# Attention of the next batch inside the feed-forward stream: windowed attention and SwiGLU in one kernel

## Chip, cores and metric

One core of one Trainium2 chip. The metric is the device time of one execution in microseconds (us), median over runs.

## What is computed

```python
# q, k, v: (4, 8, 768, 64) float32 = batch B, heads H, sequence S, head width D
scores = (q @ k^T) / sqrt(64) + bias            # per batch and head
# key j is kept for query i if j < 8 (global) or 0 <= i - j < 96 (local)
# bias = -slope[h] * (96 if global and not local, else i - j); other keys: -1e9
a = softmax(scores)
x = (a @ v) with heads side by side             # (3072 tokens, 512)
g = x @ w_gate                                  # w_gate, w_val: (512, 1536)
out = ((g * sigmoid(g)) * (x @ w_val)) @ w_out  # w_out: (1536, 512); out: (3072, 512) float32
```

## The kernel before

Matmul operands are fp16, accumulation is float32 in PSUM. There are two stages, one after the other, each with its own PSUM pool (`psA`, then `psB`).

**Attention** runs over the 4 batches and over 4 pairs of heads in each. The loads of q, k and v go out on POOL's queue (`issue_in_dmas`) and cast to fp16 on the way; a row of a q or k load is 64 floats, 256 bytes. A batch has 16 q and k loads of 768 such rows and one v load of 6,144. The three weights follow the loads of batch 1. For a pair, `issue_qk_transposes` turns q and k with 12 matmuls against the identity (L150, L153), and VectorE copies the two results out of PSUM (L156, L157); this is done one pair ahead. Scores are computed transposed, keys on the partitions: per head six tiles of a chunk of 128 keys by up to 256 queries (L200, L205) and one of the first chunk by the last 512 queries (L209), for the 8 global keys. ScalarE takes the exponential (L221, L223, L225), VectorE multiplies with a mask of exponentials of the bias (L229). For the sums, the attention weights are the stationary operand and v with a column of ones the moving one (L236), which gives 6 blocks of 128 queries by 65 columns; VectorE takes reciprocals (L243) and products (L244). `issue_x_transposes` turns the result again (L164) into `xT`, feature-major, for the next stage (L166).

**Feed-forward** runs over 6 tiles of 512 tokens. For each of 12 blocks of 128 hidden features: 4 gate matmuls (L259), 4 value matmuls (L264), a sigmoid on ScalarE (L269), and two products on VectorE (L271, L272). Then 4 blocks of 128 tokens get 12 output matmuls each (L276), an eviction on ScalarE (L281) and a store (L282).

The order on each engine is planned by the framework's scheduler.

## Time and profile before

| | us |
|---|---|
| median of 3 runs | 361.26 (360.68 to 361.34) |
| span of the profiled execution, first to last instruction | 357.6 |
| up to the first transpose | 12.0 |
| attention | 153.8 |
| feed-forward, first to last matmul | 187.9 |
| after the last matmul | 3.9 |

Over the span TensorE is busy for 308.0 us, VectorE for 175.4, ScalarE for 126.5, POOL for 64.8. Busy times are sums over stages that have different limits, so the stages are to be read one by one. The granted TensorE clock is a share of 2.4 GHz; 0.50 is 1.2 GHz.

### The profile page before, as it was taken

What the parts mean: (1) busy time and instruction counts of PE and PEld (TensorE: products, weight loads), DVE (VectorE), ACT (ScalarE), POOL (GpSimd) and SP (SyncE); (2) the same over time, 40 slices, a digit from 0 to 9 for tenths busy, and PEclk for the clock granted to TensorE, in tenths of its full rate; (3) what the DMA queues carried; (4) which work ended last, traced back from release to release, by engine and by line L of the source; (5) the groups of instructions that cost most, each with busy time, mean ns of one, the idle gap of its engine ahead of it and who ended that gap; (6) DMA issues with size and microseconds to landing.
All of it is one profiled execution on the core that took longest, in us unless ns stands there. A gap on an engine that the chain in (4) does not pass through costs nothing.

```text
span 357.6 us, 4597 instructions
## 1 busy us (share of the span) xinstructions
PE 308.0 (86%) x1856; PEld 160.9 (45%) x1856; DVE 175.4 (49%) x288; ACT 126.5 (35%) x194; POOL 64.8 (18%) x76
## 2 busy tenths in 40 slices
PE   0447888787888788776999999999999999999995
PEld 0325555455555455443444444444444444444442
DVE  0217555535555555542871575178158418706740
ACT  1125444434444544533331332333133233313321
POOL 7659560195920000000000000000000000000000
PEclk9999555556555655555999999999999999999999
DMA  7999999999990000000001100200110020011002
GB/s 292 165 122 115 127 198 211 194 124 132 119 122 1 2 0 2 0 2 0 0 2 59 60 0 22 98 0 2 59 59 2 29 88 2 1 73 46 0 29 89
DMA packets 81333, 23.66 MB, mean 66 GB/s; under 512 B 75552, under 2 KB 77088, under 8 KB 81184
## 3 DMA queue, kind: packets, MB, share of 16 engines
q0 software_dynamic: 77424, 14.16, 71.3%
q1 hardware_dynamic: 3888, 9.21, 6.9%
q8 instruction: 14, 0.23, 0.3%
q14 instruction: 7, 0.06, 0.1%
HBM read 31.23 MB, written 6.29 MB: 105 GB/s over the span
## 4 chain that ended last, share of the span: by engine, by line
PE 53%; DVE 1%; ACT 1%; issue 0%; ACTq 0%
PE gps L259 18%; PE vps L264 17%; PE ops L276 17%; ACT AT L221 0%; PE outq L236 0%; DVE AT L229 0%; PE xtp L164 0%; ACT osb L281 0%; DVE xT L166 0%; DVE xs L244 0%; ACT AT L223 0%; PE scB L205 0%; PE scB L209 0%; DVE rqi L243 0%; ACTq L281 0%
## 5 line engine op out<-in xcount | busy, mean ns | idle before, releaser
L271 DVE TENSOR_TENSOR sl<-gps,sg 128x512 f32<-128x512 f32 x72 | 49.7, 691 | 72.0 <-ACT sg L269 71.9
L259 PE MATMUL gps<-xT,wg 128*128 128x512 f16 x288 | 74.8, 383 | 0.6 <-DVE xT L166 0.6
L264 PE MATMUL vps<-xT,wv 128*128 128x512 f16 x288 | 74.3, 381 | 0.0
L269 ACT ACTIVATE sg<-gps 128x512 f32<-128x512 f32 x72 | 43.0, 597 | 74.8 <-PE gps L259 74.8
L276 PE MATMUL ops<-wo,hT 128*128 128x512 f16 x288 | 63.1, 379 | 0.0
L272 DVE TENSOR_TENSOR hT<-vps,sl 128x512 f16<-128x512 f32 x72 | 49.7, 692 | 7.6 <-PE gps L259 0.5
L221 ACT ACTIVATE AT<-scA 128x1024 f16<-128x1024 f32 x32 | 32.7, 1023 | 53.4 <-issue 35.2
L259 PEld LDWEIGHTS <-wg 128*128 128x128 f16 x288 | 28.3, 98 | 34.9 <-issue 1.4
L264 PEld LDWEIGHTS <-wv 128*128 128x128 f16 x288 | 28.3, 98 | 34.6 <-issue 1.1
L276 PEld LDWEIGHTS <-hT 128*128 128x128 f16 x288 | 28.2, 98 | 34.0
L200 PE MATMUL scA<-qk 64*128 64x256 f16 x128 | 31.3, 390 | 11.2 <-ACT AT L225 10.6
L150 PE MATMUL trq<-ident,qst 128*128 128x128 f16 x96 | 14.8, 295 | 25.3 <-DMA qst<-in_q_dram 18.2
L229 DVE TENSOR_TENSOR AT<-AT,masks 128x1408 f16<-128x1408 f16 x32 | 28.5, 890 | 11.8 <-ACT AT L223 11.8
L281 ACT COPY osb<-ops 128x512 f32<-128x512 f32 x24 | 14.0, 585 | 53.5 <-PE ops L276 53.5
L108 POOL DMA_DIRECT2D kst<-in_k_dram x32 | 27.4, 879 | 28.4 <-DMA vpp<-in_v_dram 15.1
L236 PE MATMUL outq<-vpp,AT 128*128 128x65 f16 x480 | 30.8, 238 | 1.8 <-DVE AT L229 1.5
L236 PEld LDWEIGHTS <-AT 128*128 128x128 f16 x480 | 26.4, 127 | 11.7 <-DVE AT L229 6.8
L223 ACT ACTIVATE AT<-scB 128x384 f16<-128x384 f32 x32 | 15.7, 490 | 39.7 <-PE scB L209 39.7
L108 POOL DMA_DIRECT2D qst<-in_q_dram x32 | 27.3, 883 | 6.3 <-DMA wg<-in_moe_w_gate_dram 5.4
L243 DVE RECIPROCAL rqi<-outq 128x6 f32<-128x6 f32 x32 | 6.3, 196 | 38.7 <-PE outq L236 38.7
L150 PEld LDWEIGHTS <-qst 128*128 128x128 f16 x96 | 9.6, 127 | 34.0 <-DMA qst<-in_q_dram 19.1
L200 PEld LDWEIGHTS <-qk 64*128 64x128 f16 x128 | 14.3, 121 | 22.0 <-issue 16.0
(24 smaller groups left out, 169.4 us busy)
## 6 DMA issues: line engine op xcount, KB each, us to landing
out_dram<-osb SPq DMA_DIRECT2D x24, 256.0 KB, 2.0
qst<-in_q_dram POOLq DMA_DIRECT2D x32, 96.0 KB, 9.6
kst<-in_k_dram POOLq DMA_DIRECT2D x32, 96.0 KB, 9.3
vpp<-in_v_dram POOLq DMA_DIRECT2D x4, 768.0 KB, 11.5
masks<-attn_masks SPq DMA_DIRECT2D x1, 2816.0 KB, 9.4
wg<-in_moe_w_gate_dram POOLq DMA_DIRECT2D x1, 1536.0 KB, 11.8
wv<-in_moe_w_val_dram POOLq DMA_DIRECT2D x1, 1536.0 KB, 18.4
wo<-in_moe_w_out_dram POOLq DMA_DIRECT2D x1, 1536.0 KB, 25.3
```

The lines of the kernel that those rows point to most:

```text
L108: nc.gpsimd.dma_start(out=st[:, hp, :, hi, :], in_=src[b, 2 * hp + hi].rearrange("(j p) d -> p j d", p=128))
L150: nc.tensor.transpose(trq[:, 128 * j:128 * j + 128], qst4[:, hp, j, :], ident)
L200: nc.tensor.matmul(scA[:, col:col + n], lhsT=kT[:, 128 * ck:128 * ck + 128], rhs=qT[:, q0:q0 + n], start=True, stop=True)
L221: nc.scalar.activation(out=AT[:, 0:1024], in_=scA, func=AF.Exp, scale=float(scale))
L229: nc.vector.tensor_mul(AT[:, 0:1408], AT[:, 0:1408], masks[:, h, :])
L236: nc.tensor.matmul(oq3[:, jq, :], lhsT=AT[:, at_col:at_col + 128], rhs=vpp[:, bh * NT + ck, 0:65], start=(i == 0), stop=(i == len(cl) - 1))
L259: nc.tensor.matmul(gps, lhsT=wg[:, c, 128 * f:128 * f + 128], rhs=xT[c][:, 512 * tb:512 * tb + 512], start=(c == 0), stop=(c == NC - 1))
L264: nc.tensor.matmul(vps, lhsT=wv[:, c, 128 * f:128 * f + 128], rhs=xT[c][:, 512 * tb:512 * tb + 512], start=(c == 0), stop=(c == NC - 1))
L269: nc.scalar.activation(out=sg, in_=gps, func=AF.Sigmoid)
L271: nc.vector.tensor_mul(sl, gps, sg)
L272: nc.vector.tensor_mul(hT[:, f, :], vps, sl)
L276: nc.tensor.matmul(ops, lhsT=hT[:, f, 128 * t4:128 * t4 + 128], rhs=wo[:, f, :], start=(f == 0), stop=(f == NFF - 1))
```

## The change

Everything in the kernel is new but the loops' arithmetic.

- **Order.** The scheduler's order is replaced by the order written in the program (`manual_schedule`). Batch 0's attention runs first, in 12 rounds in which up to three pairs take one step each. From then on the program is a row of 96 slots: a slot has the 8 gate and value matmuls of one block of one 384-token tile (`gate_val`), three output matmuls of the tile before (`out_part`), and one step of attention of the next batch (`attention`), two steps ahead of the slot number. A pair has six steps: transposes, three of scores, two of values. Batches 1 to 3 have 72 steps, two of which stand ahead of slot 0.
- **Loads.** q and k are loaded with 6 tokens a partition, so that a row is 1,536 bytes; a q or k load of one batch is split at first (2, 2 and 4 heads) and whole later. v comes in 7 chunks plus 7 small loads. The weights are loaded in parts. All stay on POOL's queue: q and k of batch 0 for four heads, v of batch 0, the other four heads, wg and wv in four parts, wo in three, q and k of batch 1, v of batch 1. Those of batches 2 and 3 stand in the slots.
- **Chunks of keys.** A chunk is 8 global keys and 120 keys in order, against a window of 216 queries; there are 7. Global keys count for the first 120 queries of a window, so each query meets them once. The seven windows lie in three banks of 432 columns, and the two heads of a pair are computed in turn, one on each half of the array's rows.
- **Masks** are made on the chip, by the exponential of a table of distances, 864 columns a head, before and during batch 0's attention.
- **Values.** v (or a block of ones) is stationary with 64 columns, the weights move, and the two heads write the two halves of the partitions. The result is already feature-major, and the second transposes fall away. The sums of weights come out 64 times; VectorE transposes them in blocks of 32, takes 11 or 13 reciprocals, and transposes back.
- **Engines.** In the stream POOL multiplies with the masks and with the reciprocals (after a copy of the numerator by ScalarE); in batch 0 VectorE does. ScalarE copies q out of PSUM.
- **Gate.** Sigmoid becomes tanh: (tanh(g/2) + 1) * g in one VectorE instruction, and the factor of a half is in the eviction.

The core of the diff (added lines and lines in common):

```diff
+    def load_qk(b, h0, h1):
+        for st, src in ((qst[b], q), (kst[b], k)):
+            nc.gpsimd.dma_start(
+                out=st[:, h0:h1, :],
+                in_=src[b, h0:h1].rearrange("h (p j) d -> p h (j d)", p=128))
+    def load_v(b, c):
+        if c < NCH:
+            n = min(KC, S - KC * c)
+            nc.gpsimd.dma_start(
+                out=vS[NG:NG + n, b, c, :, :],
+                in_=v[b, :, KC * c:KC * c + n, :].rearrange("h p d -> p h d"))
+        else:
+            for cc in range(NCH):
                 nc.gpsimd.dma_start(
+                    out=vS[0:NG, b, cc, :, :],
+                    in_=v[b, :, 0:NG, :].rearrange("h p d -> p h d"))
...
+    def load_w(g):
+        f0 = WF * g
+        for w, src in ((wg, moe_w_gate), (wv, moe_w_val)):
             nc.gpsimd.dma_start(
+                out=w[:, :, f0:f0 + WF],
+                in_=src[:, f0:f0 + WF].rearrange("(c p) f -> p c f", p=128))
+    def load_wo(g):
+        nc.gpsimd.dma_start(
+            out=wo[:, 4 * g:4 * g + 4, :],
+            in_=moe_w_out[512 * g:512 * g + 512].rearrange("(f p) d -> p f d", p=128))
+    xT = sb.tile([128, NC, TOK], FP16, name="xT")
+    attn_tags = ["a0", "a1", "a2"]
+    pro_tags = ["a0", "a1", "a2", "g0", "g1", "v0", "v1", "o0"]
+    state = {"tags": pro_tags, "n": 0}
...
+    def make_masks(h):
+        nc.scalar.activation(out=masks[:, h, :], in_=dist, func=AF.Exp, scale=-slopes[h])
...
+        def transposes(self):
+            b, hp = self.b, self.hp
+            trq = bank("trq", FP16, S)
+            trk = bank("trk", FP16, S)
+            for st, tr in ((qst[b], trq), (kst[b], trk)):
+                for j in range(J):
+                    for hi in range(2):
+                        nc.tensor.transpose(
+                            tr[64 * hi:64 * hi + 64, 128 * j:128 * j + 128],
+                            st[:, 2 * hp + hi, D * j:D * j + D], ident)
+            self.qT = sb2.tile([128, S], FP16, name="qT", tag="qT")
+            self.kT = kTs[hp % 2]
+            nc.scalar.copy(
+                out=self.qT.rearrange("r (p j) -> r p j", j=J),
+                in_=trq.rearrange("r (j p) -> r p j", j=J))
+            k3 = self.kT.rearrange("r (c m) -> r c m", m=128)
+            t3 = trk.rearrange("r (j p) -> r p j", j=J)
+            for c0, c1, n in ((0, 6, KC), (6, 7, S - 6 * KC)):
+                nc.vector.tensor_copy(
+                    out=k3[:, c0:c1, NG:NG + n].rearrange("r c (p j) -> r c p j", j=J),
+                    in_=t3[:, 20 * c0:20 * c0 + (c1 - c0) * (n // J), :].rearrange(
+                        "r (c p) j -> r c p j", c=c1 - c0))
+            nc.vector.tensor_copy(
+                out=k3[:, :, 0:NG],
+                in_=k3[:, 0, NG:2 * NG].unsqueeze(1).broadcast_to([128, NCH, NG]))
+        def scores(self, bk, mul_eng):
+            hp = self.hp
+            sc = [bank("scA"), bank("scB")]
+            for c in range(NCH):
+                cb, col, q0, n = chunks[c]
+                if cb != bk:
+                    continue
+                for hi in range(2):
+                    r = slice(64 * hi, 64 * hi + 64)
+                    nc.tensor.matmul(
+                        sc[hi][:, col:col + n],
+                        lhsT=self.kT[r, 128 * c:128 * c + 128],
+                        rhs=self.qT[r, q0:q0 + n], start=True, stop=True)
             for hi in range(2):
+                at = sb2.tile([128, BANK], FP16, name="at", tag=f"at{hi}{bk}")
+                nc.scalar.activation(out=at, in_=sc[hi][:, 0:BANK], func=AF.Exp, scale=scale)
+                self.at[hi, bk] = at
             for hi in range(2):
+                at = self.at[hi, bk]
+                mul_eng.tensor_mul(at, at, masks[:, 2 * hp + hi, WIN * bk:WIN * bk + BANK])
+        def values(self, half, norm):
+            b, hp = self.b, self.hp
+            lo, hi_q = HALF[half]
+            n_q = hi_q - lo
+            num = bank("num")
+            den = bank("den")
+            parts = []
+            for c in range(NCH):
+                cb, col, q0, n = chunks[c]
+                a, z = max(q0, lo), min(q0 + n, hi_q)
+                if a < z:
+                    parts.append((c, cb, col + a - q0, a - lo, z - a))
+            for dst, ones_side in ((den, True), (num, False)):
+                for i, (c, cb, col, o, n) in enumerate(parts):
+                    for hi in range(2):
+                        r = slice(64 * hi, 64 * hi + 64)
                         nc.tensor.matmul(
+                            dst[r, o:o + n],
+                            lhsT=ones if ones_side else vS[:, b, c, 2 * hp + hi, :],
+                            rhs=self.at[hi, cb][:, col:col + n],
+                            start=(i == 0), stop=(i == len(parts) - 1),
+                            skip_group_check=True)
+            dT = sb2.tile([128, 416], FP32, name="dT", tag="dT")
+            dR = sb2.tile([128, 13], FP32, name="dR", tag="dR")
+            rb = sb2.tile([128, 416], FP32, name="rb", tag="rb")
+            nb = n_q // 32
+            nc.vector.transpose(dT[:, 0:n_q], den[:, 0:n_q])
+            nc.vector.reciprocal(
+                out=dR[:, 0:nb], in_=dT[:, 0:n_q].rearrange("p (n i) -> p n i", i=32)[:, :, 0])
+            nc.vector.transpose(
+                rb[:, 0:n_q].rearrange("p (n i) -> p n i", i=32),
+                dR[:, 0:nb].unsqueeze(2).broadcast_to([128, nb, 32]))
+            dst = xT[:, hp, b * S + lo:b * S + hi_q]
+            if norm == "vector":
+                nc.vector.tensor_mul(dst, num[:, 0:n_q], rb[:, 0:n_q])
+            else:
+                ns = sb2.tile([128, 416], FP32, name="ns", tag="ns")
+                nc.scalar.copy(out=ns[:, 0:n_q], in_=num[:, 0:n_q])
+                nc.gpsimd.tensor_mul(dst, ns[:, 0:n_q], rb[:, 0:n_q])
+    hTs = {}
+    def gate_val(t, f):
+        if f == 0:
+            hTs[t] = sb2.tile([128, NFF, TB], FP16, name="hT", tag="hT")
+        gps = ps.tile([128, 512], FP32, name="gps", tag=f"g{f % 2}")
+        vps = ps.tile([128, 512], FP32, name="vps", tag=f"v{f % 2}")
+        for w, dst in ((wg, gps), (wv, vps)):
             for c in range(NC):
                 nc.tensor.matmul(
+                    dst[:, 0:TB], lhsT=w[:, c, 128 * f:128 * f + 128],
+                    rhs=xT[:, c, TB * t:TB * t + TB],
                     start=(c == 0), stop=(c == NC - 1))
+        th = sb2.tile([128, TB], FP32, name="th", tag="th")
+        nc.scalar.activation(out=th, in_=gps[:, 0:TB], func=AF.Tanh, scale=0.5)
+        sl = sb2.tile([128, TB], FP32, name="sl", tag="sl")
+        nc.vector.scalar_tensor_tensor(
+            out=sl, in0=th, scalar=1.0, in1=gps[:, 0:TB], op0=AluOp.add, op1=AluOp.mult)
+        nc.vector.tensor_mul(hTs[t][:, f, :], vps[:, 0:TB], sl)
+    ops_t = {}
+    def out_part(t, i, part):
+        if part == 0:
+            ops_t[0] = ps.tile([128, 512], FP32, name="ops", tag="o0")
+        ops = ops_t[0]
+        for f in range(3 * part, 3 * part + 3):
+            nc.tensor.matmul(
+                ops, lhsT=hTs[t][:, f, 128 * i:128 * i + 128], rhs=wo[:, f, :],
+                start=(f == 0), stop=(f == NFF - 1))
+        if part == 3:
             osb = sb2.tile([128, DM], FP32, name="osb", tag="osb")
+            nc.scalar.mul(out=osb, in_=ops, mul=0.5)
+            r0 = TB * t + 128 * i
+            nc.sync.dma_start(out=out[r0:r0 + 128, :], in_=osb)
+    stage(0)
+    load_qk(0, 0, 2)
+    load_qk(0, 2, 4)
+    for c in range(NCH + 1):
+        load_v(0, c)
+    load_qk(0, 4, 8)
+    for g in range(4):
+        load_w(g)
+    for g in range(3):
+        load_wo(g)
+    stage(1)
+    load_qk(1, 0, 8)
+    for c in range(NCH + 1):
+        load_v(1, c)
+    pairs = {(b, hp): Pair(b, hp) for b in range(B) for hp in range(NP)}
+    make_masks(0)
+    make_masks(1)
+    for t in range(6 + 2 * (NP - 1)):
+        for hp in range(NP):
+            s = t - 2 * hp
+            if 0 <= s < 6:
+                if s == 1 and hp + 1 < NP:
+                    make_masks(2 * hp + 2)
+                    make_masks(2 * hp + 3)
+                pairs[0, hp].step(s, nc.vector, "vector")
+    state["tags"] = attn_tags
+    state["n"] = 0
+    todo = [(b, hp, s) for b in range(1, B) for hp in range(NP) for s in range(6)]
+    AHEAD = 2
+    loads = {}
+    for b in range(2, B):
+        base = 24 * (b - 2) + 2
+        loads[base] = [lambda b=b: (stage(b), load_qk(b, 0, 8))]
+        for c in range(NCH + 1):
+            loads.setdefault(base + 1 + c, []).append(lambda b=b, c=c: load_v(b, c))
+    def attention(i):
+        if i < len(todo):
+            b, hp, s = todo[i]
+            pairs[b, hp].step(s, nc.gpsimd, "gpsimd")
+    for i in range(AHEAD):
+        attention(i)
+    NT = TOK // TB
+    for t in range(NT):
+        for f in range(NFF):
+            i = NFF * t + f
+            for fn in loads.get(i, []):
+                fn()
+            gate_val(t, f)
+            if t > 0:
+                out_part(t - 1, f // 4, f % 4)
+            attention(i + AHEAD)
+    for i in range(3):
+        for part in range(4):
+            out_part(NT - 1, i, part)
 # ---- launch: one core; inputs and outputs as the reference has them ----
 _INS = ['q', 'k', 'v', 'n_global', 'n_local', 'moe_w_gate', 'moe_w_val', 'moe_w_out']
 _OUTS = [((3072, 512), 'float32')]
 _NUMBERS = {'n_global': 8, 'n_local': 96}
```

## Rows read from the trace of the kernel before

**Rows 1.** The page's slices, 40 of 8.94 us: busy tenths, granted clock in tenths.

```profile
PE   0447888787888788776999999999999999999995
PEclk9999555556555655555999999999999999999999
DMA  7999999999990000000001100200110020011002
```

**Rows 2.** Stretches: length, busy us (instructions) of PE, PEld, DVE, ACT, POOL; clock; DMA.

```profile
0.00:12.00 12.00, 0.00 (x0) 0.00 (x0) 0.00 (x0) 1.28 (x1) 7.17 (x13) 1.00 1.05 268
12.00:165.80 153.80, 120.16 (x993) 76.34 (x994) 76.22 (x144) 66.91 (x96) 57.59 (x64) 0.60 1.63 91
165.80:353.70 187.90, 187.82 (x864) 84.60 (x863) 99.22 (x144) 57.73 (x97) 0.00 (x0) 0.99 0.09 33
353.70:357.60 3.90, 0.00 (x0) 0.00 (x0) 0.00 (x0) 0.58 (x1) 0.00 (x0) 0.79 0.19 69
```

**Rows 3.** The chain that ended last, feed-forward: start us, us, what.

```profile
186.99 0.86 PE vps L264 x4
187.86 10.36 PE ops L276 x48
```

**Rows 4.** POOL in order of time: start us, us, instruction, [idle before, releaser].

```profile
1.24 1.78 POOL L108 DMA_DIRECT2D qst<-in_q_dram  x2 [0.80 <-POOLq L301]
...
23.66 0.83 POOL L108 DMA_DIRECT2D kst<-in_k_dram  x1 [3.97 <-DMA vpp<-in_v_dram]
...
43.33 0.82 POOL L108 DMA_DIRECT2D kst<-in_k_dram  x1 [3.79 <-DMA vpp<-in_v_dram]
...
56.23 0.82 POOL L108 DMA_DIRECT2D qst<-in_q_dram  x1 [5.41 <-DMA wg<-in_moe_w_gate_dram]
63.63 0.82 POOL L108 DMA_DIRECT2D kst<-in_k_dram  x1 [6.58 <-DMA wv<-in_moe_w_val_dram]
71.24 0.82 POOL L108 DMA_DIRECT2D kst<-in_k_dram  x1 [6.79 <-DMA wo<-in_moe_w_out_dram]
```

**Rows 5.** All engines in order of time, at half clock.

```profile
37.02 0.83 PE L153 MATMUL trk<-ident,kst 128*128 128x128 f16 x6
```

**Rows 6.** Weight loads of TensorE in order of time, at full clock.

```profile
28.35 0.33 PEld L200 LDWEIGHTS <-qk 64*128 64x128 f16 x4 [0.18 <-PE outq L236]
28.89 0.17 PEld L150 LDWEIGHTS <-qst 128*128 128x128 f16 x3 [0.21 <-issue]
...
29.35 0.55 PEld L236 LDWEIGHTS <-AT 128*128 128x128 f16 x15
...
30.90 0.34 PEld L164 LDWEIGHTS <-xs 128*128 128x128 f16 x6 [0.57 <-DVE xs L244]
31.34 0.09 PEld L200 LDWEIGHTS <-qk 64*128 64x128 f16 x1
```

**Rows 7.** Groups by line: count | busy us, mean ns | idle before, releaser.

```profile
L221 ACT ACTIVATE AT<-scA 128x1024 f16<-128x1024 f32 x32 | 32.7, 1023 | 53.4 <-issue 35.2 <-PE scA L200 15.9 <-ACT AT L225 2.2
...
L229 DVE TENSOR_TENSOR AT<-AT,masks 128x1408 f16<-128x1408 f16 x32 | 28.5, 890 | 11.8 <-ACT AT L223 11.8
...
L244 DVE TENSOR_TENSOR xs<-outq,rqi 128x384 f16<-128x384 f32 x32 | 17.8, 557 | 1.1
...
L223 ACT ACTIVATE AT<-scB 128x384 f16<-128x384 f32 x32 | 15.7, 490 | 39.7 <-PE scB L209 39.7
...
L281 ACT COPY osb<-ops 128x512 f32<-128x512 f32 x24 | 14.0, 585 | 53.5 <-PE ops L276 53.5
...
L156 DVE COPY qk<-trq 128x768 f16<-128x768 f16 x16 | 8.9, 557 | 24.5 <-PE trq L150 14.1 <-PE scB L209 10.4
...
L243 DVE RECIPROCAL rqi<-outq 128x6 f32<-128x6 f32 x32 | 6.3, 196 | 38.7 <-PE outq L236 38.7
...
L269 ACT ACT_TABLE_LOAD x1 | 1.3, 1283 | 5.7 <-PE gps L259 5.7
...
L119 POOL MEMSET vpp<- 128x192 f16 x1 | 1.0, 975 | 0.0
```

More of the change, by code (lines that the diff above doesn't have):

```diff
@@ L14, with _build_dist @@
 AF = mybir.ActivationFunctionType
-MASK_NEG = -30000.0
-def _build_consts(B, H, S, D, NG, NL):
-    slopes = 2.0 ** (-8.0 * (np.arange(H, dtype=np.float64) + 1) / H)
-    kk = np.arange(128)[:, None]
-    qq = np.arange(256)[None, :]
-    rel = qq - kk
-    is_local = (rel >= 0) & (rel < NL)
-    is_glob = kk < NG
-    keep0 = is_local | is_glob
-    dist0 = np.where(is_local, np.abs(rel), float(NL))
-    keepb = is_local
-    distb = np.abs(rel)
-    big = np.zeros((128, H, 1408), np.float16)
-    for h in range(H):
-        m0 = (np.exp(-slopes[h] * dist0) * keep0).astype(np.float16)
-        mb = (np.exp(-slopes[h] * distb) * keepb).astype(np.float16)
-        big[:, h, 0:256] = m0
-        for c in range(4):
-            big[:, h, 256 + 256 * c:512 + 256 * c] = mb
-        big[:, h, 1280:1408] = mb[:, 0:128]
-    bias0b = np.full((128, H), MASK_NEG, np.float32)
-    for h in range(H):
-        bias0b[:NG, h] = -float(NL) * slopes[h]
-    ident = np.eye(128, dtype=np.float16)
-    return big, bias0b, ident
+FAR = 60000.0
+KC = 120
+WIN = 216
+BANK = 432
+def _build_dist(S, NG, NL):
+    row = np.arange(128)[:, None]
+    col = np.arange(WIN)[None, :]
+    key = row - NG
+    rel = col - key
+    local = (rel >= 0) & (rel < NL) & (key >= 0)
+    inner = np.where(local, rel, FAR)
+    inner = np.where((row < NG) & (col < KC), NL, inner)
+    first = np.where(local, rel, FAR)
+    first = np.where(~local & (key >= 0) & (key < NG) & (col < KC), NL, first)
+    d = np.concatenate([first, inner, inner, inner[:, :168], inner[:, :48]], axis=1)
+    return d.astype(np.float16)
 @with_exitstack
@@ L69 @@
     assert (NG, NL) == (8, 96)
-    NT = S // 128
-    NBH = B * H
     NP = H // 2
@@ L118 @@
-    issue_in_dmas(0)
-    nc.gpsimd.memset(vpp[:, :, 64:65], 1.0)
-    xT = [sb.tile([128, TOK], FP16, name=f"xT{c}", tag=f"xT{c}") for c in range(NC)]
+    dist = sb.tile([128, 2 * BANK], FP16, name="dist")
+    nc.sync.dma_start(out=dist, in_=dist_dr.ap())
+    masks = sb.tile([128, H, 2 * BANK], FP16, name="masks")
+    ones = sb.tile([128, 64], FP16, name="ones")
+    nc.vector.memset(ones, 1.0)
+    kTs = [sb.tile([128, NCH * 128], FP16, name=f"kT{i}") for i in range(2)]
+    for t in kTs:
+        nc.vector.memset(t[:, 6 * 128 + 56:], 0.0)
@@ new lines, with stage @@
+    vS = sb.tile([128, B, NCH, H, D], FP16, name="vS")
+    nc.vector.memset(vS[:, :, 6, :, :], 0.0)
+    qst, kst = {}, {}
+    def stage(b):
+        qst[b] = sb2.tile([128, H, J * D], FP16, name="qst", tag="qst")
+        kst[b] = sb2.tile([128, H, J * D], FP16, name="kst", tag="kst")
+    def load_qk(b, h0, h1):
[3 more added lines that the diff above has]
+                in_=src[b, h0:h1].rearrange("h (p j) d -> p h (j d)", p=128))
@@ new lines, in load_wo, with bank @@
+    def load_wo(g):
[6 more added lines that the diff above has]
+    state = {"tags": pro_tags, "n": 0}
+    def bank(name, dt=FP32, cols=512):
+        tags = state["tags"]
+        tag = tags[state["n"] % len(tags)]
+        state["n"] += 1
+        return ps.tile([128, cols], dt, name=name, tag=tag)
@@ L262 @@
                     start=(c == 0), stop=(c == NC - 1))
-            for c in range(NC):
-                nc.tensor.matmul(
-                    vps, lhsT=wv[:, c, 128 * f:128 * f + 128],
-                    rhs=xT[c][:, 512 * tb:512 * tb + 512],
-                    start=(c == 0), stop=(c == NC - 1))
-            sg = sb2.tile([128, 512], FP32, name="sg", tag="sg")
-            nc.scalar.activation(out=sg, in_=gps, func=AF.Sigmoid)
-            sl = sb2.tile([128, 512], FP32, name="sl", tag="sl")
@@ L271 @@
-            nc.vector.tensor_mul(sl, gps, sg)
-            nc.vector.tensor_mul(hT[:, f, :], vps, sl)
-        for t4 in range(4):
-            ops = psB.tile([128, 512], FP32, name="ops", tag="ops")
-            for f in range(NFF):
-                nc.tensor.matmul(
-                    ops, lhsT=hT[:, f, 128 * t4:128 * t4 + 128],
-                    rhs=wo[:, f, :],
-                    start=(f == 0), stop=(f == NFF - 1))
-            osb = sb2.tile([128, DM], FP32, name="osb", tag="osb")
-            nc.scalar.copy(out=osb, in_=ops)
-            nc.sync.dma_start(
-                out=out[512 * tb + 128 * t4: 512 * tb + 128 * (t4 + 1), :],
-                in_=osb)
+        th = sb2.tile([128, TB], FP32, name="th", tag="th")
```

173 lines of the change are left out of this document (29 added, 144 removed).

## The prediction

> **What bounds the kernel now.** I read the slices first: TensorE is busy all along after the start, but its clock stands at half over most of the first half of the span, and the loads on the DMA engines end about where slice 12 does [rows 1]. The table of stretches gives the stages [rows 2]: 12.0 us of loads, 153.8 us of attention (TensorE busy for 120.2 of them, mean clock 0.60), 187.9 us of feed-forward (TensorE never idle, clock 0.99), and 3.9 us from the last matmul to the end, 357.6 in all. The runs' median is 361.26, so 3.7 us lie around the span; I add them at the end. The chain of waits shows that the feed-forward stage hangs on matmuls alone: four take 0.86 us, 48 take 10.36, so 216 ns for 512 columns [rows 3], 2.37 columns a nanosecond. Six tiles of 144 matmuls are 186.6 us of pure streaming; nothing of that can go. Attention hangs on no single engine: TensorE is idle 33.6 us there and at half clock most of the rest. What the change can win is the attention stage: three batches of four can lie inside a stage where VectorE and ScalarE idle [rows 2].
>
> **What is removed.** The 153.8 us stage as a stage, the 12.0 us wait for the first loads in part, and the second activation table load.
>
> **The start.** All loads stay on POOL's queue, and attention of batch 1 stands on TensorE ahead of the first feed-forward matmul, so the feed-forward stream begins only when batch 1's q and k have landed behind all weights. Row prices: a batch's 18,432 rows of 256 bytes (16 q and k loads of 768, one v of 6,144) take from 23.66 to 43.33, 1.07 ns a row; wo's 1,536 rows of 2,048 bytes take 7.61 us behind wv, 4.95 ns a row [rows 4]. A straight line between them gives 3.84 ns for the new 1,536-byte rows. Then: q and k of batch 0, 2,048 rows, 7.9; v, 6,592 rows of 256 bytes, 7.0; wg and wv, 4,096 rows, 15.7; wo 7.6; q and k of batch 1, 7.9: 46.1 us. From the first issue at 1.24, with some 2 us for the last landing, that is 49 to 50. POOL issues the 33 loads ahead at 0.83 each, 27 us, below that. Bounds: at wo's rate throughout 48; at the rate of the 256-byte rows 76.
>
> Batch 0's own attention starts near 6 and lies beside this. VectorE, a pair: copies 1.3 (below), six mask products at 0.38, twice two transposes, a reciprocal and a product, 3.8; 7.4, four pairs 30 us. TensorE at half clock takes 0.107 for 128 columns (six transposes in 0.83 with the tail of the last, [rows 5]), so 18 us for the 43,392 columns of four pairs if the two heads stream side by side and 36 if not. ScalarE has 23: eight masks of 864 elements at 0.89, 24 exponentials, four copies of q at 0.8. With the waits of twelve rounds I put its end at 46, not later than the loads; what hides it is the weights' transfer, and if it needs over 50 us the start moves with it. After q and k of batch 1 land, TensorE still has to transpose at half clock (24 x 0.107 = 2.6), wait for VectorE's copies (about 1.6), and do the first scores (0.4): the stream starts at **55** (bounds 53 and 80).
>
> **The stream.** Feed-forward columns are the same: 768 matmuls of 384 (162 ns) and 288 of 512 (216 ns), **186.6**. Between them lie 70 attention steps of 12 pairs. A pair has 24 transposes of 128 columns, 14 score matmuls with 2,592, and 32 value matmuls with 5,184: 10,848 columns. The trace shows matmuls only one after the other: 4.6 us at full clock, the upper bound. The two heads now use different halves of the array in turn; fully side by side it is 2.3 us, about what 70 weight loads need at the pace of the 15 loads in 0.55 (32 ns each, [rows 6]). No row says which; I take the middle, 3.45, 12 pairs 41.4, less the two steps done before: **40** (27 to 55).
>
> The Trainium skill (TensorEngine Tiling (Array Packing), Restrictions) says that column tiling does without fast weight loads; no row here has a column tile. By the Trainium skill's TensorE: Matmul & The Clock Gate (LDWEIGHTS: columns over 1.2 GHz) the 56 loads of 64 columns in a pair would be 3.0 us, an estimate, and with the scores the sum would be some 2 us more.
>
> Each step switches the array's shape twice. At full clock: four score matmuls from 28.35 stream until 28.78 and the next form loads at 28.89; six transposes from 30.90 end at 31.24 and the 64-row form loads at 31.34 [rows 6]. 0.10 each; 140 of them, **14** (12 to 28, if column tiles drain twice as long).
>
> Waits: VectorE's copies (557 ns for 768 contiguous elements; the new strided ones up to one element a cycle, 0.9, and two short ones at 0.2: 1.3) must end before the next step, 1.94 us of feed-forward later. Exponentials of 432 are 0.53, between L223's 490 ns for 384 and L221's 1,023 for 1,024; tanh of 384 is 0.49, the products of 384 are 0.56 (row L244) [rows 7]. Per pair, VectorE: 12 x 0.56, 1.3, and twice 1.3 is 10.6; ScalarE: six tanh, six exponentials, a 0.8 copy, two 0.49 copies and 1.5 evictions of 0.585 is 8.8. TensorE needs 6 x 1.94 + 3.45 + 1.2 = 16.3, so both lie beside it. POOL takes eight products a pair, six masks and two norms. Its only compute row is the strided memset, 975 ns for 192, which for 432 would be 2.2; VectorE's 890 for 1,408 would be 0.27. I take 1.3: 10.4, and with its DMA issues (32 of 0.9 over twelve pairs, 2.4) 12.8, still below 16.3. The steps that wait for POOL stand two slots, over 5 us, behind their scores. For what is late now and then (the first twelve slots have no output matmuls between, v of batch 1 lands about when it is wanted) I take half a microsecond a pair, **6** (0 to 12).
>
> At its start the clock is cold: stage 187.9 against 186.6, **1.3** [rows 2]. At the end 36 output matmuls share one bank: three evictions of about 0.85 with hand-over stand open, **2.5**. Sum: 55 + 186.6 + 40 + 14 + 6 + 1.3 + 2.5 = 305.4; the tail 3.9, around the span 3.7: **313 us**.
>
> **Rivals.**
> 1. *Loads at the price of short rows.* If 1,536-byte rows move at the rate of 256-byte ones, the stream starts at 80: 338 us. For it: the short rows carry 240 GB/s; against it: wo's 2,048-byte rows carry 413.
> 2. *POOL becomes the bound.* At 2.2 us a product, 20.0 a pair against 16.8 with waits: 12 x 3.2 more, 351 us. It bounds from 1.75 on, and eats the gain at 2.3. Against it: the memset writes single strided elements.
> 3. *Weight loads in line* (the one that ends slower). If in the tiled forms a load cannot be pulled ahead of the running matmul, each of 840 costs its 95 ns openly: 80 us, 393 us. It decides from 57 ns a load. Against it: the 64-row score loads are already pulled ahead [rows 6]; for it: no row has column tiles.
> 4. *The clock falls in the stream.* Attention ran at 0.60 though TensorE was busy for 120.2 of 153.8. Work done at half clock costs itself again; 48 us of the stream's 250 undo the gain, twice that gives 409. Against it: three quarters of the stream is feed-forward work, which held 0.99.
> 5. *Table loads in the stream.* The trace has a load of 1.283 us between exp and sigmoid. If tanh and exp share no table, each of 36 score slots has two: ScalarE 4.3 us against 2.65, 58 us, 371 us.
>
> On the last, the Trainium skill (ScalarE: Activation LUTs, Table sets: the hidden batching unit) lists tanh in exp's set, so there would be no load in the stream; no row here has a tanh.
>
> **Chances.** Forecast 0.64 (own range 300 to 330: start 53 to 60, attention 27 to 55); rival 1 0.10; rival 2 0.08, of which faster 0.06 and the same 0.01; rival 3 0.09, of which 0.01 faster and 0.01 the same, since part of the price may be hidden; rival 4 0.06, half of it faster; rival 5 0.03. Faster 0.64 + 0.10 + 0.06 + 0.01 + 0.03 = 0.84; same 0.02; slower 0.14. A measurement here tells about 0.2% from no change. The range, 290 to 345, reaches from a pair at 2.3 us with few waits to rival 1; rivals 3 and 5, most of 4 and the far end of 2 are outside.
>
> **What would show it.** Start: the first gate matmul near 55, with POOL's loads landed just before. Stream: granted clock 1.0, TensorE hardly idle, 2.4 to 3.3 us a slot, steps of a pair adding to 3 to 5 us; POOL's products at 1.0 to 1.6. One table load in the whole trace. Wrong it would be by gaps on TensorE released by POOL or by VectorE's copies, by pairs of matmuls that never overlap and loads in line, by a clock of 0.5 in the stream, or by a first gate matmul after 65.

## The result, and the profile after

The changed kernel takes **301.25 us** (median of 4 runs, 301.10 to 301.37) against 361.30 for the kernel before (4 runs, 360.68 to 362.73): a ratio of 0.833, 95% interval 0.831 to 0.835. The forecast was 313.

The slices of the page after, 40 of 7.48 us, answer to [rows 1]. TensorE is full from slice 8 on (slice 10, at 7, holds two value steps that wait), its clock is whole from there, and the loads ahead of the stream end with slice 7; slices 9 to 11 and 17 to 19 are the loads of batches 2 and 3.

```profile
PE   2528541599799999999999999999999999999983
PEclk9999755599999999999999999999999999999999
...
DMA  8989999909950010299501000100010000100111
```

The table of stretches after, cut at the first gate matmul and after the last matmul's start, answers to [rows 2] (same columns):

```profile
0.00:57.00 57.00, 23.11 (x308) 16.24 (x309) 29.40 (x75) 22.55 (x38) 32.38 (x47) 0.79 1.33 168
57.00:295.00 238.00, 233.10 (x1870) 125.27 (x1868) 149.99 (x297) 110.73 (x226) 120.51 (x133) 0.99 0.30 48
295.00:299.30 4.30, 0.33 (x2) 0.00 (x0) 0.00 (x0) 0.60 (x1) 0.00 (x0) 1.00 0.16 61
```

The span is 299.3: 57.0 of start, 238.0 of stream, 4.3 of end. In the stream TensorE is idle for 4.9 us and its clock stands at 0.99 of 2.4 GHz; VectorE (150), ScalarE (111) and POOL (121) have room. Before, 165.8 us passed ahead of the first feed-forward matmul [rows 2].

**The start.** TensorE in order of time after (start us, us, engine, line, what, [idle before, releaser]):

```profile
41.68 0.87 PE L238 MATMUL num<-at,vS 128*64 128x216 f16 x9
50.52 0.85 PE L182 MATMUL trq<-ident,qst 128*64 128x128 f16 x12 [7.97 <-DMA qst<-in_q_dram]
54.46 0.85 PE L182 MATMUL trk<-ident,kst 128*64 128x128 f16 x12 [3.09 <-DMA kst<-in_k_dram]
56.53 0.36 PE L210 MATMUL scA<-qT,kT 64*128 64x216 f16 x1 [1.22 <-DVE kT L197]
...
57.00 1.46 PE L272 MATMUL gps<-xT,wg 128*128 128x384 f16 x4
...
113.34 0.53 PE L182 MATMUL trq<-ident,qst 128*64 128x128 f16 x12
113.70 0.50 PE L182 MATMUL trk<-ident,kst 128*64 128x128 f16 x12
114.13 0.82 PE L272 MATMUL gps<-xT,wg 128*128 128x384 f16 x4
114.79 0.81 PE L272 MATMUL vps<-xT,wv 128*128 128x384 f16 x4
115.44 0.81 PE L291 MATMUL ops<-wo,hT 128*128 128x512 f16 x3
116.18 0.26 PE L210 MATMUL scA<-qT,kT 64*128 64x216 f16 x1
116.19 0.26 PE L210 MATMUL scB<-qT,kT 64*128 64x216 f16 x1
116.29 0.25 PE L210 MATMUL scA<-qT,kT 64*128 64x216 f16 x1
116.29 0.25 PE L210 MATMUL scB<-qT,kT 64*128 64x216 f16 x1
116.47 0.82 PE L272 MATMUL gps<-xT,wg 128*128 128x384 f16 x4
...
285.66 2.75 PE L291 MATMUL ops<-wo,hT 128*128 128x512 f16 x12 [0.69 <-ACT osb L296]
289.10 2.75 PE L291 MATMUL ops<-wo,hT 128*128 128x512 f16 x12 [0.69 <-ACT osb L296]
292.58 2.75 PE L291 MATMUL ops<-wo,hT 128*128 128x512 f16 x12 [0.73 <-ACT osb L296]
```

The top shows that batch 0's attention is over at about 42.5, and that TensorE then stands for 8 us until q of batch 1 has landed, and for 3 more until k has: 3.94 us between the two, for 1,024 rows, 3.85 ns a row.

**A slot.** The middle of that fence is one. Gate and value matmuls take 1.31 us (114.13 to 115.44), the output part 0.74 with a change of the array's shape behind it (116.18), a score step 0.29 (to 116.47), the transposes 0.79 (113.34 to 114.13). The scores of the two heads start 0 to 10 ns apart, and the next two 0.10 us later, about what 216 columns take alone at the feed-forward's rate (0.09, [rows 3]): the heads stream **side by side** at full rate. The start-to-start times of the six steps of a pair, each with the change back, are 0.79, 0.29, 0.29, 0.30, 0.59 and 0.79: 3.05 us. The bottom is the end: the last three output blocks wait 0.7 us each for the eviction of the bank they share.

The groups by line after, of the operations whose price had no row, or a row of another shape, in [rows 7]:

```profile
L278 ACT ACTIVATE th<-gps 128x384 f32<-128x384 f32 x96 | 47.5, 494 | 37.1 <-PE gps L272 36.7
L220 POOL TENSOR_TENSOR at<-at,masks 128x432 f16<-128x432 f16 x72 | 70.5, 1005 | 31.7 <-ACT at L216 31.6
L260 POOL TENSOR_TENSOR xT<-ns,rb 128x352 f16<-128x352 f32 (+1 forms) x24 | 24.1, 1005 | 26.1 <-DVE rb L251 26.0
L159 ACT ACT_TABLE_LOAD x1 | 1.3, 1283 | 0.7 <-PEq L376 0.7
```

POOL in order of time after, at the loads and where the stream begins:

```profile
15.15 0.55 POOL L123 DMA_DIRECT2D vS<-in_v_dram  x1 [0.60 <-DMA vS<-in_v_dram]
...
23.03 0.74 POOL L135 DMA_DIRECT2D wv<-in_moe_w_val_dram  x1 [0.59 <-DMA kst<-in_k_dram]
24.97 0.74 POOL L140 DMA_DIRECT2D wo<-in_moe_w_out_dram  x1 [1.20 <-DMA wg<-in_moe_w_gate_dram]
...
32.17 0.89 POOL L111 DMA_DIRECT2D qst<-in_q_dram  x1 [1.87 <-DMA wv<-in_moe_w_val_dram]
...
54.70 0.57 POOL L123 DMA_DIRECT2D vS<-in_v_dram  x1 [3.30 <-DMA kst<-in_k_dram]
...
59.74 1.10 POOL L123 DMA_DIRECT2D vS<-in_v_dram  x2 [0.50 <-DMA vS<-in_v_dram]
60.94 5.81 POOL L220 TENSOR_TENSOR at<-at,masks 128x432 f16<-128x432 f16 x6
```

POOL's queue issues batch 1's small loads of v until 60.84, though the first scores were there at 57, and then has six mask products in arrears. The rows up to 32.17 show how the queue is paced. In this program POOL does not issue a load before the one eight places ahead of it has landed: the 28th, at 23.03, waits for batch 0's last k, the 20th; the 29th for the first wg, the 21st; the 32nd for the second wv, the 24th. With them goes the busy share of the DMA engines over the first 60 us after, 40 slices of 1.5 us:

```profile
DMA  0699999993149999999999999999999999999994
```

It has a hole at 13.5 to 18 us. POOL is then at the end of v's seven small loads of batch 0, the last three of which wait for chunks of v to land, and the next large load, q of heads 4 to 7, is not issued before 15.70.

### The profile page after: what moved, and what is told of

Read it like the earlier page. It is cut to its first block, busy times and chain, and to the rows that moved or that the text cites. A ratio compares the mean times of both kernels' runs of the same rounds, so it can differ in the third digit from the quotient of the medians.

```text
span 299.3 us, 5659 instructions
## 1 busy us (share of the span) xinstructions
PE 256.5 (86%) x2176; PEld 141.5 (47%) x2176; DVE 179.4 (60%) x372; ACT 133.9 (45%) x265; POOL 152.9 (51%) x179
## 4 chain that ended last, share of the span: by engine, by line
PE 71%; DMA 16%; POOL 8%; DVE 2%; ACT 1%; issue 1%; POOLq 0%; ACTq 0%; DVEq 0%
PE gps L272 21%; PE ops L291 21%; PE vps L272 19%; DMA vS<-in_v_dram 7%; DMA wo<-in_moe_w_out_dram 5%; POOL at L220 3%; DMA wv<-in_moe_w_val_dram 3%; PE scA L210 3%; PE den L238 3%; PE num L238 2%; POOL vS L118 2%; PE trq L182 2%; PE trk L182 1%; POOL qst L111 1%; ACT osb L296 1%
## 5 line engine op out<-in xcount | busy, mean ns | idle before, releaser
L280 DVE SCALAR_TENSOR_TENSOR sl<-th,gps 128x384 f32<-128x384 f32 x96 | 52.9, 551 | 61.3 <-ACT th L278 61.3
L220 POOL TENSOR_TENSOR at<-at,masks 128x432 f16<-128x432 f16 x72 | 70.5, 1005 | 31.7 <-ACT at L216 31.6
L272 PE MATMUL gps<-xT,wg 128*128 128x384 f16 x384 | 79.8, 331 | 0.0
L272 PE MATMUL vps<-xT,wv 128*128 128x384 f16 x384 | 78.8, 328 | 0.0
L278 ACT ACTIVATE th<-gps 128x384 f32<-128x384 f32 x96 | 47.5, 494 | 37.1 <-PE gps L272 36.7
L282 DVE TENSOR_TENSOR hT<-vps,sl 128x384 f16<-128x384 f32 x96 | 53.5, 558 | 10.1 <-PE vps L272 0.2
L216 ACT ACTIVATE at<-scA 128x432 f16<-128x432 f32 x48 | 25.5, 532 | 37.9 <-PE scB L210 37.9
L260 POOL TENSOR_TENSOR xT<-ns,rb 128x352 f16<-128x352 f32 (+1 forms) x24 | 24.1, 1005 | 26.1 <-DVE rb L251 26.0
L118 POOL DMA_DIRECT2D vS<-in_v_dram x28 | 25.1, 909 | 10.9 <-DMA wo<-in_moe_w_out_dram 4.9
L216 ACT ACTIVATE at<-scB 128x432 f16<-128x432 f32 x48 | 25.5, 532 | 0.0
L210 PE MATMUL scA<-qT,kT 64*128 64x216 f16 (+2 forms) x112 | 18.7, 267 | 7.9 <-DVE kT L197 5.6
```

The lines of the kernel that those rows point to most:

```text
L118: nc.gpsimd.dma_start(out=vS[NG:NG + n, b, c, :, :], in_=v[b, :, KC * c:KC * c + n, :].rearrange("h p d -> p h d"))
L210: nc.tensor.matmul(sc[hi][:, col:col + n], lhsT=self.kT[r, 128 * c:128 * c + 128], rhs=self.qT[r, q0:q0 + n], start=True, stop=True)
L216: nc.scalar.activation(out=at, in_=sc[hi][:, 0:BANK], func=AF.Exp, scale=scale)
L220: mul_eng.tensor_mul(at, at, masks[:, 2 * hp + hi, WIN * bk:WIN * bk + BANK])
L260: nc.gpsimd.tensor_mul(dst, ns[:, 0:n_q], rb[:, 0:n_q])
L272: nc.tensor.matmul(dst[:, 0:TB], lhsT=w[:, c, 128 * f:128 * f + 128], rhs=xT[:, c, TB * t:TB * t + TB], start=(c == 0), stop=(c == NC - 1))
```

## The experiments

Ratios are to the kernel before, timed beside each; what a run adds or takes is told against the 301.25 us of the changed kernel.

### All matmuls of one head, then of the other

In the transposes, the scores and the values the loop over the two heads is made the outer one:

```diff
-            for c in range(NCH):
-                ...
-                for hi in range(2):
+            for hi in range(2):
+                for c in range(NCH):
```

> The matmuls of the two heads are no longer issued in turn, but all of one head and then all of the other; nothing else changes. Theory (the two heads stream side by side in the two halves of the array): the streaming of a pair goes from 10,848 / 2 columns, 2.26 us, to 4.52, so the twelve pairs of the stream cost 27 us more, 328 us, and a pair's six steps go from 3.0 to about 5.3 us. Rival (the pace of 70 weight loads at some 32 ns sets the 2.3 us, whatever the order): no change, 301 us.

Measured: 303.54 us, ratio 0.839 (0.837 to 0.842). TensorE in order of time in this kernel, one score step:

```profile
103.91 0.26 PE L210 MATMUL scA<-qT,kT 64*128 64x216 f16 x1
103.91 0.26 PE L210 MATMUL scB<-qT,kT 64*128 64x216 f16 x1
104.01 0.25 PE L210 MATMUL scA<-qT,kT 64*128 64x216 f16 x1
104.02 0.25 PE L210 MATMUL scB<-qT,kT 64*128 64x216 f16 x1
```

The program now has A, A, B, B; the trace still has A with B and, 0.10 us later, A with B. So the theory's prediction fell: the order in the program does not make the heads overlap. A matmul for one half of the array starts past an earlier one that waits for the other half. Only the steps with many matmuls lose something: the transposes take 0.93 us in place of 0.79, the longer value step 0.86 in place of 0.78. Over the stream these are 1.5 and 0.9 us. The run lost 2.3, but the two are not the same thing: its first gate matmul also came 0.7 later, and its value steps waited 1.3 less. The time is nearer the rival's 301, but the rival's cause, the pace of the weight loads, does not fit the scores: two matmuls with their loads take 0.10 us there, and two loads at 32 ns would be 0.06. For the transposes, at 33 ns each in the changed kernel, the run can't tell the two apart. The Trainium skill (TensorEngine Tiling (Array Packing), Key Properties) says that different tiles load and multiply in parallel; the 0 to 10 ns agree. The prediction's sum went by the middle of its two bounds instead.

### All attention first, in the new form

The order of the kernel before, with everything else of the change; the products with masks and reciprocals are VectorE's throughout:

```diff
+    order = [(b, hp) for b in range(B) for hp in range(NP)]
+    for t in range(6 + 2 * (len(order) - 1)):
+        for p, (b, hp) in enumerate(order):
+            s = t - 2 * p
...
-            attention(i + AHEAD)
```

> All four batches of attention run in rounds ahead of the feed-forward stream, in the new form, with the products on VectorE as batch 0 has them; the stream holds feed-forward alone. Theory (the gain is the overlap; the new form is bound by VectorE, 7.4 us a pair, and by waits when it stands alone): twelve pairs at about 8 us ahead, first gate matmul near 150, 345 us in all (335 to 355). Rival (the gain is the form: fewer columns, two heads at once): a pair at 3 to 4 us, first gate matmul near 105, 300 us.

Measured: 338.87 us, ratio 0.937 (0.934 to 0.940), as the theory had it (335 to 355). Its stretches:

```profile
0.00:142.00 142.00, 73.47 (x1120) 56.72 (x1120) 103.79 (x271) 64.53 (x121) 58.24 (x83) 0.77 0.92 105
142.00:332.60 190.60, 188.50 (x1058) 103.57 (x1056) 109.14 (x198) 60.78 (x119) 0.00 (x0) 0.99 0.09 33
```

The change falls into two parts: the new form of attention and of the loads by itself brings 22.4 us, and that it runs inside the stream 37.6. In the stage of its own TensorE has 73 us of work in 142 and VectorE 104, at a mean clock of 0.77; from 66.5 us on a pair takes 6.85 us, against 3.0 to 3.6 that a pair adds to the stream.

### Sigmoid in place of tanh

```diff
-        nc.scalar.activation(out=th, in_=gps[:, 0:TB], func=AF.Tanh, scale=0.5)
+        nc.scalar.activation(out=th, in_=gps[:, 0:TB], func=AF.Sigmoid)
...
-            out=sl, in0=th, scalar=1.0, in1=gps[:, 0:TB], op0=AluOp.add, op1=AluOp.mult)
+            out=sl, in0=th, scalar=0.0, in1=gps[:, 0:TB], op0=AluOp.add, op1=AluOp.mult)
```

> Tanh goes back to sigmoid (the VectorE product adds 0 in place of 1, the eviction multiplies by 1). Theory (exp and sigmoid lie in different tables, so each slot with scores needs two loads of 1.28 us): ScalarE's work per pair goes from 8.8 to 16.5 us and passes TensorE's 14.7; with slack pooled over a pair 22 us more, 323 us, with each score slot for itself 70 us more, 371 us; 345 in the middle, and some 70 table loads in the trace. Rival (tanh is only arithmetic, and the loads find cover or are not needed): 301 to 304 us.

Measured: 349.37 us, ratio 0.967 (0.958 to 0.975). Groups by line of ScalarE in this kernel:

```profile
L278 ACT ACT_TABLE_LOAD x36 | 46.2, 1283 | 0.6
L216 ACT ACT_TABLE_LOAD x35 | 44.9, 1283 | 0.6
```

71 loads in the stream in place of none, 91 us on ScalarE, 48 us more, near the 345 that the theory had in the middle. So the gain hangs on tanh: with sigmoid the new order would have gained 12 us in place of 60. By the Trainium skill (ScalarE: Activation LUTs, Table sets: the hidden batching unit) tanh lies in exp's set and sigmoid anchors another; the one load after and the 72 here agree.

### A second product on POOL, whole and half

Each mask product of the stream is followed by a product with ones over all 432 columns, or over 216:

```diff
+                if mul_eng is nc.gpsimd:
+                    mul_eng.tensor_mul(at, at, one432)
```

> In the stream POOL multiplies each block of attention weights a second time, by ones, so the measured 1.0 us per product is doubled for the six mask products of a pair. Theory (POOL has slack, but not twice its load): a pair needs 12 x 1.0 + 2.0 + 2.4 for its loads = 16.4 us of POOL against 14.7 of TensorE, so POOL becomes the bound: 20 us more, 322 us, with TensorE waiting for POOL. Rival (what POOL does is far enough ahead of the value matmuls that its pace is of no matter): 301 to 304 us.

> A second product by ones over 216 of the 432 columns follows each mask product on GpSimd in the stream, so that one product costs it about 1.55 us in place of 1.0. If GpSimd is held by a chain of latency (six products of a pair, then about 6.9 us by way of the values, the transposes and the next scores until its next product can start, against 14.7 to 15.4 us that the stream takes for a pair), the pair takes 6 x 1.55 + 6.9 = 16.2 us, and eleven or twelve pairs give 8 to 15 us: 309 to 316 us, with the values of the second and third slot waiting for GpSimd. If it is held by its own busy time alone (6 x 1.55 + 2 + 2.4 = 13.7 us, under 14.7), nothing shows but a little queueing: 301 to 304 us.

Measured: 355.58 us, ratio 0.984 (0.976 to 0.992), for the whole one; 325.02, ratio 0.900 (0.896 to 0.903), for the half. The first is far outside both expectations, and is where the theory of a chain of latency comes from; the second was made to test it. POOL in order of time with the half product, the end of one pair and the start of the next:

```profile
112.46 1.00 POOL L222 TENSOR_TENSOR at<-at,masks 128x432 f16<-128x432 f16 x1 [3.30 <-ACT at L218]
113.54 0.59 POOL L224 TENSOR_TENSOR at<-at,one 128x216 f16<-128x216 f16 x1
114.09 1.00 POOL L222 TENSOR_TENSOR at<-at,masks 128x432 f16<-128x432 f16 x1
...
121.69 0.59 POOL L224 TENSOR_TENSOR at<-at,one 128x216 f16<-128x216 f16 x1
122.24 0.93 POOL L264 TENSOR_TENSOR xT<-ns,rb 128x352 f16<-128x352 f32 x1
124.47 1.07 POOL L264 TENSOR_TENSOR xT<-ns,rb 128x416 f16<-128x416 f32 x1 [1.30 <-DVE rb L255]
129.05 1.00 POOL L222 TENSOR_TENSOR at<-at,masks 128x432 f16<-128x432 f16 x1 [3.51 <-ACT at L218]
```

And TensorE's group of value matmuls, 60 to 290 us of the run with the whole one:

```profile
L242 PE MATMUL den<-at,ones 128*64 128x216 f16 (+2 forms) x192 | 19.1, 255 | 38.0 <-POOL at L224 37.9
```

A pair of products comes every 1.63 us; six take 9.8 (112.46 to 122.2). The second step of value matmuls waits for the sixth product, and TensorE works in order here: the next pair's transposes stand a slot behind those values, its first scores a slot behind the transposes, then comes the exponential, and POOL has no mask product to do until 129.05, 6.8 us after its last one; the two products with reciprocals between take 2 us of that. So a pair takes 6 x 1.63 + 6.9 = 16.7; the trace has 16.4 to 16.7 from pair to pair in the six that no load of v or first slot disturbs (after: 15.36), and 18.7 to 19.4 with the whole product, where 6 x 2.03 + 6.9 is 19.1. POOL was busy in that run for 189 of 230 us: the bound is a **round trip**, not the engine's load. The period was right, the total was not (309 to 316 expected, 325 measured). The six pairs make 6.9 us of the 23.8. The first two take 17.9 each, where after they take 14.2 and 14.8, without output parts in their slots: 6.9 more. Two whose products lie between the issue of v's loads on POOL take 18.6 and 17.3: 5.1. And 3.8 are lost ahead of the first, 1.1 behind the last. The expectation had a period for all pairs and nothing for the start and for the loads.

### The mask products on VectorE

```diff
-            pairs[b, hp].step(s, nc.gpsimd, "gpsimd")
+            pairs[b, hp].step(s, nc.vector, "gpsimd")
```

> The six mask products of a pair move from POOL to VectorE in the stream, as batch 0 has them; the norm stays on POOL. Theory (TensorE bounds the stream and VectorE has room): VectorE needs 13.0 us a pair against 14.7, and the first products no longer wait behind the loads on POOL's queue: 299 to 301 us. Rival (VectorE's queue delays the copies and the gate products, and TensorE waits): 305 us or more.

Measured: 299.21 us, ratio 0.828 (0.824 to 0.833). No value step waits any more, which takes away 3.5 us, all in the first pairs. Some of it comes back: the scores of the first pairs wait 1.9 us for VectorE's copies of k, where 0.4 were waited before, and the clock is whole at 61.7 us in place of 60.8. The 2 us gained are what is left, and no run shows what POOL costs by itself.

### The order of the loads

Three runs that only move lines of the list of loads (the third also gives the last three output blocks a bank each). *wo last*: wo's three loads go behind batch 1's q, k and v. *Batch 1 early*: after the first quarter of wg and wv come q, k and v of batch 1, then the other weights. *Also batch 0 early*: and all q and k of batch 0 stand ahead of its v. The second, in short:

```diff
     load_qk(0, 4, 8)
-    for g in range(4):
-        load_w(g)
-    for g in range(3):
-        load_wo(g)
+    load_w(0)
     stage(1)
     load_qk(1, 0, 8)
     for c in range(NCH + 1):
         load_v(1, c)
+    for g in range(1, 4):
+        load_w(g)
+    for g in range(3):
+        load_wo(g)
```

> Only the order of the loads changes: wo goes behind q, k and v of batch 1. Theory (the stream's start is set by the place of batch 1's q and k in the queue): wo's 7.6 us fall away from the start, first gate matmul near 49.5, and POOL's first mask products no longer wait behind v's small loads; 292 to 294 us. Rival (the start is set by batch 0's chain of attention, or the transfers share the engines so that the order is of no matter): 300 to 302 us.

> Only the order of the loads changes: q, k and v of batch 1 go ahead of all weights but the first part of wg and wv. Theory (the queue sets the start): q and k land near 33, batch 0's attention, which ends at 42, becomes what holds the start; first gate matmul near 45 to 47, 289 to 292 us, unless the later parts of wg and wv (about 4 us each) come late for slots 3, 6 and 9. Rival (the order is of no matter): 300 to 302 us. Second rival (the weights come late for the stream): first gate matmul near 46, but gaps on TensorE released by loads of wg and wv, 295 us and more.

> On top of the loads order of e4: all q and k of batch 0 go ahead of its v (the third and fourth pair waited for them until 21.4 in e4), and the last three blocks of output matmuls take three banks in place of one. Theory (the start hangs on the order of the queue and then on batch 0's chain on VectorE, 30 us from 6; the end on three evictions): first gate matmul near 43, 1.5 us off the end, 285 to 287 us. Rival (v of batch 0, now later, holds the first values as long as q and k held the third pair): 290 to 292 us.

Measured:

| | us | ratio (95%) | first gate matmul |
|---|---|---|---|
| changed kernel | 301.25 | 0.833 (0.831 to 0.835) | 57.0 |
| wo last | 296.54 | 0.819 (0.817 to 0.821) | 50.3 |
| batch 1 early | 291.67 | 0.808 (0.804 to 0.811) | 47.5 |
| also batch 0 early | 290.02 | 0.802 (0.796 to 0.807) | 45.7 |

The second came out at the time expected, with its gate matmul at 47.5 where 45 to 47 was expected; the first gained 4.7 where 7 to 9 was expected, and the third as its rival had it. In the first the gate matmul came 6.7 us earlier, but POOL's mask products were late, and one value step of the first pairs waited until it took 3.4 us. In the third, TensorE in order of time shows the next wait:

```profile
13.16 0.66 PE L238 MATMUL den<-at,ones 128*64 128x216 f16 x6
19.49 0.77 PE L238 MATMUL num<-at,vS 128*64 128x216 f16 x6 [5.66 <-DMA vS<-in_v_dram]
```

What was moved back, v of batch 0, is now what batch 0 waits for. And the third's 1.65 us are not from the order alone: with a bank each the last 39 output matmuls take 8.58 us in place of 11.17, so 2.6 fall away at the end, and the order by itself has brought nothing that shows in the time. (The profiled execution of *batch 1 early* was its longest, 2.2 us over the median, so its 47.5 may be late.) The order alone is worth 9.6 us, by the second.

### The start spread

On top of the third, its three output banks included: v's seven small loads of a batch become one, spread by a copy on VectorE; v's first chunks go between the q and k loads of batch 0; and the mask products of the first two pairs in the stream are VectorE's.

```diff
+            nc.gpsimd.dma_start(
+                out=vS[0:NG, b, 0, :, :],
+                in_=v[b, :, 0:NG, :].rearrange("h p d -> p h d"))
...
     load_qk(0, 0, 2)
+    for c in (NCH, 0, 1, 2):
+        load_v(0, c)
     load_qk(0, 2, 4)
...
+            first = b == 1 and hp < 2
+            pairs[b, hp].step(s, nc.vector if first else nc.gpsimd, "gpsimd")
```

> Beside the order of loads of the run before (all queries and keys early, weights' first part, batch 1, the rest) the small transfers that bring the global rows of v are replaced by one transfer of a batch and copies on VectorE, v's first three chunks go ahead of the queries and keys of heads 2 to 4, and the mask products of the first two pairs of batch 1 are VectorE's. If the start is set by how early each load is issued on GpSimd's one queue, the first values of batch 0 no longer wait until 19.5 us, the first gate matmul comes at 42 to 43 us in place of 45.7, and the time is about 285 us (283 to 288). The rival: the transfers themselves or the attention's own chain set the start, the first gate stays at 45 or later, and the time is 289 us or more.

Measured: **284.20 us** (4 runs, 283.99 to 285.16), ratio 0.786 (0.784 to 0.789), 17 us below the changed kernel. TensorE in order of time:

```profile
14.69 0.67 PE L243 MATMUL den<-at,ones 128*64 128x216 f16 x6
15.14 0.67 PE L243 MATMUL num<-at,vS 128*64 128x216 f16 x6
...
40.55 0.87 PE L187 MATMUL trk<-ident,kst 128*64 128x128 f16 x11
44.07 0.36 PE L215 MATMUL scA<-qT,kT 64*128 64x216 f16 x1 [2.65 <-DVE kT L202]
...
44.54 1.46 PE L277 MATMUL gps<-xT,wg 128*128 128x384 f16 x4
```

The time is the theory's, but only partly for its reason. The wait for v is gone, yet the first gate matmul comes at 44.5, not at 42 to 43: batch 0's attention itself now sets it. TensorE has batch 1's k transposed by 41.4 and then waits 2.65 us for VectorE's copy, which stands behind the reciprocals and products of batch 0's last pair. Of the 5.8 us gained on the run before, 1.2 are the start; 5.5 are value steps of the stream that no longer wait (22.0 us in all there, 16.5 here), as in the run with the mask products on VectorE, and other steps lost 0.9 or so.

## Why the prediction was right

Faster was right, and for the reason given: three of four batches went into the stream at a few microseconds a pair. 313 was 11.75 us too long. Term by term, the measured from the trace after:

| term | predicted | measured |
|---|---|---|
| start of the stream | 55 | 57.0 |
| feed-forward columns | 186.6 | 186.6 |
| attention steps and changes of shape | 40 + 14 | 42.2 |
| waits and cold clock | 6 + 1.3 | 5.4 |
| evictions at the end | 2.5 | 2.6 |
| not put to a term | | 1.5 |
| tail | 3.9 | 4.0 |
| around the span | 3.7 | 1.95 |

Attention's 42.2 are the time of all its steps in the stream, 39.2, less 3.5 in which value steps wait, and 6.5 by which what stands in front of a step is longer (70 of 0.09: output parts, or value matmuls in the first twelve slots). Waits are those 3.5 and 1.9 that gate and value matmuls take beyond that and 1.31 us a slot, most of it at half clock. Evictions are told from start to start: each of the last three blocks starts 0.85 to 0.89 after the columns of the one before. The 1.5 are what is left of the span.

**The step that was mis-sized** is the pair: "No row says which; I take the middle, 3.45" and 0.10 for each of 140 switches, 54 us. The switches were priced about right, the streaming was not. The heads stream side by side at full rate, which was the lower bound, 2.3 us a pair, 26.3 in all where 40 was put; the six steps take 3.05 with the change back, 3.6 with both: 42.2, so 15.9 for the 140 switches where 14 was put. The upper bound (one head after the other) had no support beside the absence of a row, and the run with the heads in turn shows that even that order gives nearly all of the overlap.

**The start** was nearly right by luck: two errors cancel for the most part. The loads of batch 1's q and k ended at 54.4, not at 49 to 50. Their price was right: 3.85 ns a row where a line between two rows gave 3.84, and from about 23.0, when POOL's wait for batch 0's last k ended, to 54.4 it is 31.4 us, where weights, wo and batch 1's q and k were put at 31.2. What failed is "POOL issues the 33 loads ahead at 0.83 each, 27 us, below that". It compares the two at the end of the queue; at the 18th load the same prices give 16.2 us for POOL's issues and about 14 for the data, since seven of these loads are v's small ones, with hardly any data. Measured, POOL has issued the 18th at 15.7, 1.4 us of it in waits for v's chunks to land; the DMA engines have run dry by then, and batch 0's loads end near 23 instead of 18. Behind the landing only 2.5 us were left, not 5, since q was transposed while k was still on its way, and k's transposes take 0.85, with the two heads side by side. Batch 0's attention was over at 42.5 (46 predicted), so what bounds the start is the order of the loads, as *wo last* and *batch 1 early* show, which changed nothing else.

**Around the span** is an error of method: 3.7 was the median of other executions less the span of the profiled one. In the changed kernel's profiled execution, 301.1 against a span of 299.3, it is 1.8, and it is 1.74 to 1.85 in each of the ten experiments. The table's 1.95 is the median less that span.

**The rivals.** 1 (price of short rows): no, 3.85 ns a row. 2 (POOL the bound): its product costs 1.005 us, so it is not; but its threshold was wrong. "It bounds from 1.75 on" was worked out from busy time; by the round trip a product of (15.36 - 6.9) / 6 = 1.4 us begins to cost, 1.2 in the first pairs, an estimate from the two runs with the second product. By it the pair at the upper bound of 2.2 would have been 20.1, where the prediction has 20.0 by another sum: luck. 3 (weight loads in line): no. The 24 transposes, each with a load of its own, take 0.79 us with a change of shape, 33 ns for one. Nor does the time show the 2 us that the rule on fast weight loads and column tiles would have added; the Trainium skill (TensorEngine Tiling (Array Packing), Restrictions) may be right on it, but a pair's 24 loads for the transposes lie within the same 0.79 us as their matmuls. 4 (the clock falls): no, 0.99 over the stream. TensorE's clock was at 1.2 GHz from 33.5 us, inside batch 0's attention, stayed there over idle times of 8.0, 3.1 and 1.2 us, and was at 2.4 from 60.8 to the last matmul; the first slot's gate matmuls take 1.26 us in place of 0.66, about 2 us in all. 5 (table loads): no with tanh; with sigmoid it happens and costs 48, not 58.

What stays open: the 1.5 us that are put to no term, 1.3 of which are the 14 ns a slot by which eight gate and value matmuls take longer (1.31 us) than their columns alone (1.296), with no reason shown; and what a pair would take if its heads could not overlap, since no run kept them apart.

## What to carry to other kernels

When work is hidden in another stage's stream, price it by what it adds to the bounding engine there, and look for the round trips: an engine in order, that waits for a helper, that waits for the engine's next piece, is bound by the sum of the loop long before the helper is busy. Ask next what the first piece of the stream waits for: here the order of some thirty loads on one queue was worth 9.6 us on top of the change's 60, and 17 together with fewer small loads, three output banks at the end (2.6) and the first mask products on VectorE. And compare an execution's time with its own span, not with the median of others.

## What the runs showed of the hardware

- Matmuls for different halves of the array start 0 to 10 ns apart and pass one another: with four score matmuls issued A, A, B, B the first B starts with the first A, 0.10 us ahead of the second A. That a matmul with 64 columns or 64 rows streams at full rate beside its twin, loads included (3.05 us for a pair's 70 matmuls, six changes back included), was the better half of what had been allowed for.
- A change of the array's shape costs 0.09 us at full clock (output part 0.65 us alone, 0.74 with an attention step behind it), also with column tiles.
- POOL multiplies 128x432 fp16 in 1.005 us, and 128x216 in 0.59; VectorE takes 0.377 for the larger.
- With longer waits of TensorE for POOL its clock was at 1.2 GHz in more stretches: in the run with the whole second product, with 38.0 us of such waits, its mean over 60 to 290 us is 0.92; with the half product, 18.0 us, it is 0.98, and after 1.00.
- A small load of v, 8 KB, still takes POOL 0.55 to 0.63 us to issue, where one of 120 KB and more takes 0.72 to 1.00. In the kernel after, the first eighteen loads keep POOL from 1.25 to 15.7 us, and the DMA engines run dry.
